# Row loads in a lane of their own in an induced-attention and leaky-FFN kernel

## The chip, the core and the metric

The kernel runs on one core of one Trainium2 chip. The metric is device time in microseconds (us), from launch to end. Engines are named as in the profile: PE is TensorE's matmul, PEld its weight load, DVE VectorE, ACT ScalarE, POOL GpSimd, SP the SyncE queue that issues the DMAs.

## The reference, cut to what matters

```python
B, N, m, C = (4, 12480, 32, 128)          # x: B x N x C, inducing: m x C, d_ff = 2048
def mab(q, kv):
    s = scale * (q @ kv.transpose(0, 2, 1))
    s = s - s.max(-1, keepdims=True)
    a = np.exp(s)
    a /= a.sum(-1, keepdims=True) + 1e-09
    return a @ kv
h = mab(I, x)                             # 32 inducing rows look at all 12480 rows of a block
attn = mab(x, h)                          # every row looks back at the 32 rows of h
hid = attn.reshape(B * N, 128) @ w_in
out = np.maximum(0.01 * hid, hid) @ w_out
```

All is float32. The first `mab` of a block needs x twice: transposed for the scores, and as rows for the values product `a @ kv`.

## The kernel before, in words

**The long loop.** The output is made in 98 tiles of 512 tokens (one of 384), each in 16 steps of 128 hidden columns: 1568 steps. A step is four matmuls of 512 columns on PE: the hidden product `ph` (L686), and three products into `po` (L725) from `ghi` and `glo`, a high and a low part of the activated hidden values. ACT makes `ghi` (L699), DVE makes `glo` (L707). The product `ph` runs three steps ahead (`LOOK`), through three buffers. The tiles of block b stand one block after the other, and the attention of block b+1 is woven in between the steps of block b. Since PE takes its queue in order, anything in this queue that waits holds all that stands behind it.

**The lanes.** `for u in range(WOVEN, NT * NF)` issues a step and then calls `step()` on generators: `stores` (outputs), `stacking` (copies of the weights `A` for the coming tiles), `seconds` (the second softmax), `scores` (`first_scores`) and `values` (`after_h`). A generator runs to its next `yield`. A yield of `HEAVY` (15) adds to `debt`, which falls by 5 in a step (6 while tiles of block 0 run); while it is above zero, most lanes stand still. `scores` and `values` also run only every second step.

**A block's first `mab`.** Its rows lie in six groups of 2048 and a small one of 192 (`RG`), visited in three passes, `PASSES = [[RG, 0, 1], [2, 3], [4, 5]]`. `first_scores` loads x for the scores, already in blocks of 32 columns (tile `xc`, by `load_blocks`, L227: 8 DMAs for half a group, 12 for the small group, three such sets at the start of a block: 28 DMAs), transposes on DVE, and at a visit makes the scores `s_ps`, their maxima (`peaks`), the running maximum `nm` and the exponentials on ACT (`running`, L303). `first_values` loads the same x as rows (tile `xr`, by `load_rows`, L217, one DMA of 256 KB for a quarter of a group, 16 buffers), turns the exponentials (tile `ay`), and marks the pass `ready`. `value_products` (L416) multiplies `ay` with the rows into `h_ps`: 64 matmuls, 66 where the small group takes part. It is called for pass p-1 in the visit of pass p, and for the last pass out of `first_values`.

**What sets the order around the row loads.** All these DMAs are issued by SP in the order in which the generators emitted them. In `first_values` the loads of a pass stand in the generator just ahead of its exponentials: `load_rows` and a `yield` for each quarter, then the wait until `(b, p)` is in `summed`, then the turning. `scores` begins the next block, with its 28 loads, as soon as it has made its last pass.

Of the kernel before, what the change touches and what calls it, by code (L numbers as in the profile page):

```python
# [20 lines left out]
def induced_attention_then_leaky_ffn(  # L21
# [103 lines left out]

    ring = set()
    PASSES = [[RG, 0, 1], [2, 3], [4, 5]]
    scores, early, ready, summed = [], {}, set(), {}
    rows_live, rows_made = set(), [0]
    waiting = []  # L130

    xT, xr, ex, aT, A4, hw, maxima, sums_of = {}, {}, {}, {}, {}, {}, {}, {}

# [77 lines left out]
    def load_rows(b, g, q):  # L211

        _, J, K = GROUPS[g]
        n = min(K, 4)
        t = row_tile("xr", (b, g, q))
        src = rows_of(b, g).rearrange("(p k) c -> p k c", k=K)
        nc.sync.dma_start(t[: 32 * J, :n, :], src[:, 4 * q : 4 * q + n, :])  # L217
        xr[b, g, q] = t

    def load_blocks(b, g, j0, nj):  # L220

# [49 lines left out]
    def running(b, p, rm):  # L271
        gs = PASSES[p]
        n = len(gs)
        nm_old = maxima.get(b)
        nm = sb.tile([P, 1], F32, tag="nm", name="nm", bufs=3)
        four = sb.tile([M, 12], F32, tag="rd", name="four", bufs=2)
        al = None
        for j in range(4):
            nc.gpsimd.tensor_scalar_mul(four[:, n * j : n * j + n], rm[32 * j : 32 * j + 32], -SCALE)
        yield  # L280
        if nm_old is None:
            nc.vector.tensor_reduce(out=nm[:M], in_=four[:, : 4 * n], op=ALU.min, axis=AX.X)
        else:
            least = sb.tile([M, 12], F32, tag="least", name="least", bufs=2)
            nc.vector.tensor_scalar(
                out=least[:, : 4 * n], in0=four[:, : 4 * n], scalar1=nm_old[:M], scalar2=None,
                op0=ALU.min, op1=ALU.min, accum_out=nm[:M],
            )
        for j in range(1, 4):
            nc.gpsimd.tensor_copy(nm[32 * j : 32 * j + 32], nm[:M])  # L290
        maxima[b] = nm
        yield
        if nm_old is not None:
            al = sb.tile([P, 1], F32, tag="al", name="al", bufs=4)
            nc.scalar.activation(al, nm_old, AF.Exp, bias=nm, scale=-1.0)
        zg = sb.tile([P, 3], F32, tag="zg", name="zg", bufs=2)
        if RG in gs:
            nc.vector.memset(zg[:, :1], 0.0)
        for i, g in enumerate(gs):
            _, J, K = GROUPS[g]  # L300
            w, rows = 32 * K, 32 * J
            e = ex[b, g]
            nc.scalar.activation(  # L303
                e[:rows, :w], e[:rows, :w], AF.Exp, bias=nm[:rows], scale=SCALE,
                accum_out=zg[:rows, i : i + 1],
            )
            if g != RG:
                yield
        zs = sb.tile([P, 1], F32, tag="zs", name="zs", bufs=2)
        nc.vector.tensor_reduce(out=zs, in_=zg[:, :n], op=ALU.add, axis=AX.X)  # L310
        if al is not None:
            old, one = sums_of[b], zs
            zs = sb.tile([P, 1], F32, tag="zn", name="zn", bufs=2)
            nc.vector.tensor_scalar(
                out=zs, in0=old, scalar1=al, scalar2=one, op0=ALU.mult, op1=ALU.add
            )
        sums_of[b] = zs
        summed[b, p] = al
# [20 lines left out]
    def first_scores(b):  # L339


        halves = [(RG, 0, 3)] + [(g, j0, 2) for g in range(RG) for j0 in (0, 2)]
        blocks = {}

        def more():
            if halves:
                h = halves.pop(0)
                blocks[h] = load_blocks(b, *h)

        for _ in range(3):  # L350
            more()
        yield from idle(10 if b > 1 else 4)
        for p, gs in enumerate(PASSES):
            for g in gs:
                _, J, K = GROUPS[g]
                w = 32 * K
                if g == RG:
                    xT[b, g] = t = sb.tile([P, J, w], F32, tag="xTr", name="xTr", bufs=2)
                else:
                    while len(ring) == RING:  # L360
                        yield
                    ring.add((b, g))
                    xT[b, g] = t = sb.tile([P, J, w], F32, tag="xT", name="xT", bufs=RING)
                for j in range(J):
                    if g == RG:
                        if j:
                            continue
                        nc.vector.transpose(
                            t.rearrange("p j w -> p (j w)"),
                            blocks[RG, 0, 3][:, : J * K, :].rearrange("p n c -> p (n c)"),  # L370
                        )
                    else:
                        blk = blocks[g, j - j % 2, 2][:, (j % 2) * K : (j % 2 + 1) * K, :]
                        nc.vector.transpose(t[:, j, :], blk.rearrange("p n c -> p (n c)"))  # L374
                    yield HEAVY
                    if j % 2 or g == RG:
                        more()
            while p and (b, p - 1) not in ready:
                yield
            while b - 1 not in hw or hw[b - 1][2] is None or not room(2):  # L380
                yield
            if p:
                value_products(b, p - 1)
            for q in [waiting.pop(0) for _ in range(min(2, len(waiting)))]:
                ps = gen_ps("s2_ps")
                second_scores(b - 1, q, ps)
                turned(b - 1, q, ps)
            sps = {}
            for g in gs:
                if g == RG:  # L390
                    sps[g] = ps_s.tile([P, TOK], F32, tag="hp", name="s1_ps")
                else:
                    sps[g] = aux_ps("s1_ps")
                for j in range(GROUPS[g][1]):
                    columns_product(sps[g], indT, b, g, j)
            rm = peaks(b, p, sps)
            yield HEAVY
            yield from running(b, p, rm)
            yield

# [36 lines left out]

    def first_values(b):

        todo = quarters(b)  # L440
        hacc = None
        for p, gs in enumerate(PASSES):
            for _ in range(sum(max(1, GROUPS[g][2] // 4) for g in gs)):
                while not room():
                    yield
                load_rows(*todo.pop(0))
                yield
            while (b, p) not in summed:
                yield
            for g in gs:  # L450
                _, J, K = GROUPS[g]
                rows = 32 * J
                e = ex.pop((b, g))
                if g == RG:
                    ay = sb.tile([P, K, M], F32, tag="ayr", name="ayr", bufs=1)
                else:
                    ay = sb.tile([P, 16, M], F32, tag="ay", name="ay", bufs=2)
                nc.vector.transpose(ay[:rows, :K, :].rearrange("p k m -> p (k m)"), e[:rows, : 32 * K])
                ays[b, g] = ay
                yield HEAVY if g != RG else 0  # L460
            ready.add((b, p))
            if p == len(PASSES) - 1:
                value_products(b, p)
                yield
            while (b, p) not in hps:
                yield
            hacc = gathered(b, p, hacc)
            yield
        rz = sums(b)
        yield  # L470
        yield from normalise(b, hacc, rz)
# [136 lines left out]
    def stack(tiles_, engine=None):  # L608
# [22 lines left out]
        for t, parts in tiles_:  # L631
            A4[t] = a4 = sb.tile([P, TOK], F32R, tag="A4", name="A4", bufs=A4_BUFS)
            to = 0
            for b, g, js in parts:
                w, o = 32 * GROUPS[g][2], at[b, g]
                for j in js:
                    for r in range(4):
                        nc.sync.dma_start(  # L638
                            a4[32 * r : 32 * r + 32, to : to + w].bitcast(F32),
                            (ahi, alo)[r % 2][32 * j : 32 * j + 32, o : o + w].bitcast(F32),  # L640
                        )
                    to += w
                yield

    tiles = []
    PAIR_AT = 4
# [25 lines left out]
            return tile_, tile_  # L672
        return tile_.rearrange("p (n a) -> p a n", a=2), tile_.rearrange("p (a n) -> p a n", a=2)

    live, accs = {}, {}
    slots = [
        (t, f) for f0 in range(0, NF, TURN) for t in range(QUICK) for f in range(f0, f0 + TURN)
    ]
# [116 lines left out]
                debt[0] += got  # L795

    def after_h(b):
        yield from first_values(b)
        yield from expand_weights(b)
        yield from expand_linear(b)  # L800
# [381 lines left out]
    with tc.manual_schedule():  # L1182
# [14 lines left out]
        for u in range(WOVEN, NT * NF):  # L1197
# [4 lines left out]
            ffn_second(u)  # L1202
            if f == NF - 1:
                stores.append(store(t))
            debt[0] = max(0, debt[0] - (5 if b else 6))
            if not debt[0]:
                step(stores)
            step(stacking)
            if not debt[0]:
                step(seconds)  # L1210
            if u >= max(due[0], 52) and not debt[0]:
# [44 lines left out]
```

## Time and profile before

| | us |
|---|---|
| median of 3 runs | 1544.31 (1543.95 to 1544.94) |
| the profiled execution | 1542.42 |
| its span, first to last instruction | 1540.2 |
| PE busy in the span | 1485.9 (96%) |
| DVE busy | 1267.2 (82%) |
| ACT busy | 1002.0 (65%) |
| POOL busy | 112.7 (7%) |

The median compares kernels; the profile tells where the time lies in one execution. Its span is 2.2 us shorter than its own time. PE's busy share is high because nearly all its work is one dense stream of equal matmuls; its idle time is best found by asking what it waited for, and then by looking at the queue it waited on.

### The profile page before, as it was taken

The numbers are of one execution on the slowest core, as the hardware profiler recorded it, in microseconds if no ns is written. First come the engines' busy times: TensorE is split into PE (matmuls) and PEld (weight loads), VectorE is DVE, ScalarE is ACT, GpSimd is POOL, SyncE is SP. The second block draws the span as 40 slices with busy tenths as digits, with TensorE's granted clock in tenths as the row PEclk, the third lists the DMA queues.
The fourth block names the chain that finished last, engine by engine and source line by source line (L and its number), as shares of the span: only waits on it lengthen the run. The fifth ranks groups of instructions, "written<-read, shape, count | busy, mean of one in ns | idle before, by whom it ended". The sixth has DMA issues, their size and how long they took to land.

```text
span 1540.2 us, 22252 instructions
## 1 busy us (share of the span) xinstructions
PE 1485.9 (96%) x7861; PEld 1261.3 (82%) x7861; DVE 1267.2 (82%) x2137; ACT 1002.0 (65%) x1748; POOL 112.7 (7%) x182
## 2 busy tenths in 40 slices
PE   8999999969999999599999999999999999999998
PEld 6788888858789787387888888888888898888887
DVE  7889889748889797398889888888888888888886
ACT  6666767636676565276766666766766666666665
POOL 1200100000110100010100100000001000000000
PEclk9999999989999999799999999999999999999999
DMA  8136543343435343344443233112212122122211
GB/s 277 42 68 113 106 83 76 90 88 59 83 77 90 74 88 76 57 79 89 87 91 77 69 76 76 41 22 48 43 21 52 23 39 49 33 37 41 42 28 21
DMA packets 402079, 105.23 MB, mean 68 GB/s; under 512 B 372624, under 2 KB 375088, under 8 KB 401968
## 3 DMA queue, kind: packets, MB, share of 16 engines
q1 hardware_dynamic: 401920, 103.80, 32.9%
q8 instruction: 62, 1.02, 0.3%
q14 instruction: 49, 0.40, 0.1%
q10 hardware_dynamic: 48, 0.02, 0.0%
HBM read 48.94 MB, written 25.56 MB: 48 GB/s over the span
## 4 chain that ended last, share of the span: by engine, by line
PE 90%; SPq 3%; DMA 2%; DVE 2%; ACT 1%; issue 1%; POOL 0%; DVEq 0%; ACTq 0%
PE po L725 63%; PE ph L686 22%; PE s_ps L241 2%; SPq L227 2%; DMA xr<-in_x_dram 2%; PE po L744 1%; PE h_ps L416 1%; DVE glo L707 1%; DMA raw<-in_moe_w_out_dram 0%; ACT ghi L699 0%; DMA raw<-in_moe_w_in_dram 0%; SPq L772 0%; ACT e L303 0%; SPq L638 0%; PE hw_ps L527 0%
## 5 line engine op out<-in xcount | busy, mean ns | idle before, releaser
L699 ACT ACTIVATE ghi<-ph 128x512 fp32r<-128x512 f32 (+1 forms) x1568 | 930.9, 596 | 504.3 <-PE ph L686 499.1
L707 DVE SCALAR_TENSOR_TENSOR glo<-ph,ghi 128x512 fp32r<-128x512 f32 (+1 forms) x1568 | 1043.7, 680 | 230.2 <-ACT ghi L699 207.8
L686 PE MATMUL ph<-A,hws 128*128 128x512 f32 (+1 forms) x1600 | 598.7, 378 | 4.9 <-DVE glo L707 4.5
L725 PE MATMUL po<-ghi,w_hi 128*128 128x512 f32 (+1 forms) x1568 | 594.5, 379 | 0.0
L725 PE MATMUL po<-glo,w_hi 128*128 128x512 f32 (+1 forms) x1568 | 593.7, 379 | 0.0
L725 PE MATMUL po<-ghi,w_lo 128*128 128x512 f32 (+1 forms) x1568 | 593.5, 379 | 0.0
L686 PEld LDWEIGHTS ph<-A,hws 128*128 128x128 f32 x1600 | 302.4, 189 | 66.0 <-DVE glo L707 12.4
L725 PEld LDWEIGHTS po<-glo,w_hi 128*128 128x128 f32 x1568 | 296.9, 189 | 42.1 <-DVE glo L707 0.7
L725 PEld LDWEIGHTS po<-ghi,w_lo 128*128 128x128 f32 x1568 | 296.7, 189 | 41.3
L725 PEld LDWEIGHTS po<-ghi,w_hi 128*128 128x128 f32 x1568 | 297.0, 189 | 39.9 <-ACT ghi L699 0.2
L754 DVE STREAM_TRANSPOSE osb<-po 128x512 f32<-128x512 f32 (+1 forms) x98 | 68.9, 703 | 1.5 <-PE po L744 1.5
L626 POOL TENSOR_TENSOR alo<-aT,ahi 128x512 fp32r<-128x512 f32 x22 | 28.2, 1280 | 573.7 <-ACT ahi L621 516.4
L416 PE MATMUL h_ps<-xr,ay 128*32 128x128 f32 x576 | 20.6, 287 | 36.2 <-DMA xr<-in_x_dram 36.1
L374 DVE STREAM_TRANSPOSE xT<-xc 128x512 f32<-128x512 f32 x72 | 50.5, 702 | 0.0
L416 PEld LDWEIGHTS h_ps<-xr,ay 128*32 128x32 f32 x576 | 14.9, 112 | 42.1 <-DMA xr<-in_x_dram 39.1
L579 POOL TENSOR_TENSOR y<-y,mx 128x512 f32<-128x512 f32 x23 | 24.2, 1051 | 257.5 <-DVE mx L577 202.8
L744 PE MATMUL po<-A,m2s 128*128 128x512 f32 (+1 forms) x100 | 37.1, 374 | 0.0
L594 POOL TENSOR_TENSOR y<-y,sm 128x512 f32<-128x512 f32 x23 | 24.2, 1050 | 174.2 <-DVE sm L592 143.3
L334 DVE STREAM_TRANSPOSE y<-s_ps 128x512 f32<-128x512 f32 x22 | 15.7, 715 | 13.7 <-PE s_ps L241 12.2
L241 PE MATMUL s_ps<-xT,indT 128*32 128x512 f32 x192 | 24.2, 595 | 0.5 <-ACT xT L851 0.5
L241 PE MATMUL s_ps<-xT,hT 128*32 128x512 f32 x192 | 24.0, 597 | 0.4 <-ACT hT L993 0.4
L744 PEld LDWEIGHTS po<-A,m2s 128*128 128x128 f32 x100 | 18.9, 189 | 2.6
(152 smaller groups left out, 370.0 us busy)
## 6 DMA issues: line engine op xcount, KB each, us to landing
xr<-in_x_dram SPq DMA_DIRECT2D x96, 256.0 KB, 4.4
out_dram<-osb SPq DMA_DIRECT2D x384, 64.0 KB, 2.2
xc<-in_x_dram SPq DMA_DIRECT2D x288, 64.0 KB, 2.7
A<-ahi SPq DMA_DIRECT2D x188, 64.0 KB, 2.0
A<-alo SPq DMA_DIRECT2D x188, 64.0 KB, 2.0
hws<-hilo SPq DMA_DIRECT2D x64, 64.0 KB, 2.0
raw<-in_moe_w_in_dram SPq DMA_DIRECT2D x4, 512.0 KB, 7.6
raw<-in_moe_w_out_dram SPq DMA_DIRECT2D x4, 512.0 KB, 8.3
```

The lines of the kernel that those rows point to most:

```text
L227: nc.sync.dma_start(t[32 * cb : 32 * cb + 32, j * K : (j + 1) * K, :], src[:, j0 + j, :, 32 * cb : 32 * cb + 32],)
L241: nc.tensor.matmul(dst, lhsT, rhs, start=True, stop=True)
L374: nc.vector.transpose(t[:, j, :], blk.rearrange("p n c -> p (n c)"))
L416: nc.tensor.matmul(hp[32 * k : 32 * k + 32, :C], ay[:rows, 4 * q + k, :], xb[:rows, k, :], start=(i == 0 and q == 0), stop=(last[k] == i a ...
L579: engines[0].tensor_tensor(out=yv, in0=yv, in1=mx[:rows, :K].unsqueeze(2).broadcast_to([rows, K, M]), op=ALU.subtract,)
L626: (engine or nc.gpsimd).tensor_tensor(out=alo[sl], in0=aT.pop((b, g))[: 32 * J, :], in1=ahi[sl].bitcast(F32), op=ALU.subtract,)
L686: nc.tensor.matmul(ph[:, o : o + w], hw[b][1][:, f * P : (f + 1) * P], woven(A4[t][:, o : o + w], t), start=True, stop=True,)
L699: nc.scalar.activation(halves(ghi[:, :n], t)[1], live[u][2], AF.Relu)
L707: nc.vector.scalar_tensor_tensor(out=halves(glo[:, :n], t)[1], in0=ph, scalar=0.0, in1=halves(ghi[:, :n], t)[1].bitcast(F32), op0=ALU.max, ...
L725: nc.tensor.matmul(accs[t][:, :n], w[:, f, :], woven(r[:, :n], t), start=(f == 0 and w is w_hi and r is live[u][0]), stop=False,)
L744: nc.tensor.matmul(accs[t][:, o : o + w], hw[b][2], woven(a4[:, o : o + w], t), start=False, stop=(o + w == n),)
L754: nc.vector.transpose(osb[:, :n], po[:, :n])
```

## The change

`first_values` no longer loads rows. A new generator `fetch` does, in a lane `fetches` that is stepped on odd steps from 52 on, whatever `debt` is. It emits the nine loads of the first pass of a block as soon as `after_h` begins, and the sixteen of the two other passes after the second visit of that block, each where one of the 16 buffers is free. `fetched` keeps the step of a pass's last load, and `landed` says whether all loads of a pass were emitted at least `LAND` (12) steps ago; a values product now waits for that in the planner. In `running` the memset of `zg` moves to the front, one more `yield` stands between the running maximum and the first `Exp`, and the small group's `Exp` gets a yield too. The visit waits for two free row buffers only if two second products wait. `debt` falls by 4 (5 in block 0) in a step, and a stack ends with three idle steps.

```diff
+    PASS_OF = {g: p for p, gs in enumerate(PASSES) for g in gs}
+    LAND = 12
...
+    visited, fetched, now = set(), {}, [0]
...
         xr[b, g, q] = t
+        fetched[b, PASS_OF[g]] = now[0]
+
+    def fetch(b):
+
+        for p, gs in enumerate(PASSES):
+            while p and (b, 1) not in visited:
+                yield
+            for g in gs:
+                for q in range(max(1, GROUPS[g][2] // 4)):
+                    while not room():
+                        yield
+                    load_rows(b, g, q)
+                    yield
+
+    def landed(b, p):
+
+        n = sum(max(1, GROUPS[g][2] // 4) for g in PASSES[p])
+        return sum((b, g, q) in xr for g in PASSES[p] for q in range(4)) == n and now[0] >= fetched[b, p] + LAND
...
         nm_old = maxima.get(b)
+        zg = sb.tile([P, 3], F32, tag="zg", name="zg", bufs=2)
+        if RG in gs:
+            nc.vector.memset(zg[:, :1], 0.0)
...
         yield
+        yield
         if nm_old is not None:
...
-        zg = sb.tile([P, 3], F32, tag="zg", name="zg", bufs=2)
-        if RG in gs:
-            nc.vector.memset(zg[:, :1], 0.0)
...
-            if g != RG:
-                yield
+            yield
...
-            while p and (b, p - 1) not in ready:
+            while p and not ((b, p - 1) in ready and landed(b, p - 1)):
                 yield
-            while b - 1 not in hw or hw[b - 1][2] is None or not room(2):
+            while b - 1 not in hw or hw[b - 1][2] is None or not room(min(2, len(waiting))):
                 yield
...
+            visited.add((b, p))
             rm = peaks(b, p, sps)
...
-        todo = quarters(b)
         hacc = None
         for p, gs in enumerate(PASSES):
-            for _ in range(sum(max(1, GROUPS[g][2] // 4) for g in gs)):
-                while not room():
-                    yield
-                load_rows(*todo.pop(0))
-                yield
...
             if p == len(PASSES) - 1:
+                while not landed(b, p):
+                    yield
                 value_products(b, p)
...
+        yield from idle(3)
...
     def after_h(b):
+        fetches.append(fetch(b))
         yield from first_values(b)
...
-            debt[0] = max(0, debt[0] - (5 if b else 6))
+            debt[0] = max(0, debt[0] - (4 if b else 5))
...
+            now[0] = u
+            if u >= 52 and u % 2:
+                step(fetches)
```

How the instructions stand on the engines, before and now. In the names `xr` is a load of rows, `xc` a load of x for the scores, `A` a copy for a coming tile, `out_dram` a store. A row with xN at its end stands for N in a row. The change's line numbers are those of its own file.

SP, block 1, last loads of rows before the block's last values product; before:

```order
L217 DMA xr<-in_x_dram 128x512 x3
L772 DMA out_dram<-osb 256x2x32 x4
L217 DMA xr<-in_x_dram 128x512 x5
L772 DMA out_dram<-osb 256x2x32 x4
L227 DMA xc<-in_x_dram 32x2x32 x12
L227 DMA xc<-in_x_dram 32x16x32 x16
L217 DMA xr<-in_x_dram 128x512 x3
L638 DMA A_4268<-ahi 32x512
```

Three of the rows' loads stand behind the 28 loads of the next block. SP, block 1, the sixteen loads of the passes two and three; now:

```order
L248 DMA xc<-in_x_dram 32x16x32 x24
L791 DMA out_dram<-osb 256x2x32 x4
L220 DMA xr<-in_x_dram 128x512 x4
L791 DMA out_dram<-osb 256x2x32 x4
L220 DMA xr<-in_x_dram 128x512 x8
L791 DMA out_dram<-osb 256x2x32 x4
L220 DMA xr<-in_x_dram 128x512 x4
L248 DMA xc<-in_x_dram 32x16x32 x8
```

All sixteen now stand ahead of the block's own last `xc` loads. Farther down the same queue, the 28 loads of the next block; now:

```order
L656 DMA A_3533<-alo 32x512
L791 DMA out_dram<-osb 256x2x32 x12
L248 DMA xc<-in_x_dram 32x2x32 x12
L248 DMA xc<-in_x_dram 32x16x32 x16
L791 DMA out_dram<-osb 256x2x32 x4
```

The next load of rows in the queue belongs to block 2. SP, block 2, the same place; before:

```order
L217 DMA xr<-in_x_dram 128x512
L638 DMA A_7594<-ahi 32x512
L638 DMA A_7594<-alo 32x512
L638 DMA A_7594<-ahi 32x512
L638 DMA A_7594<-alo 32x512
L227 DMA xc<-in_x_dram 32x2x32 x12
L227 DMA xc<-in_x_dram 32x16x32 x16
L217 DMA xr<-in_x_dram 128x512 x3
L772 DMA out_dram<-osb 256x2x32 x8
```

and now, the last load of rows of block 2:

```order
L791 DMA out_dram<-osb 256x2x32 x8
L248 DMA xc<-in_x_dram 32x16x32 x8
L791 DMA out_dram<-osb 256x2x32 x4
L220 DMA xr<-in_x_dram 128x512
L791 DMA out_dram<-osb 256x2x32 x4
L656 DMA A_7482<-ahi 32x512
```

Sixteen copies `A` and twelve stores stand between it and the 28 `xc` loads of block 3. ACT, the exponentials of the first pass of block 2 (`er` is the small group, `y` the second softmax of block 1); before:

```order
L621 CAST ahi<-aTr 96x64 x2
L699 ACTIVATE ghi<-ph 128x512 x9
L303 ACTIVATE er,zg<-er,nm 96x64
L303 ACTIVATE e,zg<-e,nm 128x512
L699 ACTIVATE ghi<-ph 128x512 x2
L585 ACTIVATE y<-y 128x512
L303 ACTIVATE e,zg<-e,nm 128x512
L699 ACTIVATE ghi<-ph 128x512 x25
```

and now:

```order
L639 CAST ahi<-aTr 96x64 x2
L718 ACTIVATE ghi<-ph 128x512 x10
L325 ACTIVATE er,zg<-er,nm 96x64
L718 ACTIVATE ghi<-ph 128x512
L603 ACTIVATE y<-y 128x512
L718 ACTIVATE ghi<-ph 128x512
L325 ACTIVATE e,zg<-e,nm 128x512
L718 ACTIVATE ghi<-ph 128x512 x4
L325 ACTIVATE e,zg<-e,nm 128x512
```

At least one `ghi` now stands between any two of the extra activations.

## Rows read from the trace of the kernel before

**Rows 1.** The page: busy time of PE, and PE's clock in 40 slices.

```profile
PE 1485.9 (96%) x7861; PEld 1261.3 (82%) x7861; DVE 1267.2 (82%) x2137; ACT 1002.0 (65%) x1748; POOL 112.7 (7%) x182
PEclk9999999989999999799999999999999999999999
```

**Rows 2.** Waits of PE: engine, line, releaser, us in total, times, longest.

```profile
PE h_ps L416 <- DMA xr<-in_x_dram: 36.1, 5, 20.8
PE ph L686 <- DVE glo L707: 4.5, 8, 1.4
```

**Rows 3.** Stretches: length; busy PE, PEld, DVE, ACT, POOL; PEclk; DMA share; GB/s.

```profile
320.08:336.25 16.17, 3.20 (x65) 1.64 (x65) 0.57 (x1) 0.35 (x1) 1.92 (x5) 0.66 0.66 138
336.25:339.45 3.20, 3.20 (x13) 2.58 (x10) 1.35 (x3) 1.20 (x2) 0.00 (x0) 0.56 0.18 44
503.80:508.39 4.59, 2.19 (x66) 1.65 (x67) 0.69 (x1) 0.06 (x1) 0.00 (x0) 1.00 0.63 144
613.00:637.01 24.01, 3.19 (x65) 1.64 (x64) 0.69 (x1) 0.06 (x1) 0.00 (x0) 0.62 0.43 84
637.01:640.02 3.01, 3.01 (x13) 2.47 (x9) 1.31 (x2) 1.07 (x2) 0.00 (x0) 0.60 0.00 0
878.52:880.30 1.78, 1.78 (x66) 1.78 (x69) 0.69 (x1) 0.06 (x1) 0.01 (x1) 1.00 0.00 0
804.23:806.00 1.77, 1.77 (x66) 1.77 (x67) 0.69 (x1) 0.05 (x1) 0.00 (x0) 1.00 0.17 39
```

**Rows 4.** Timeline of SP's issues around the first stall: start, us, queue, line.

```profile
311.01 18.84 SPq L227 DMA_DIRECT2D xc<-in_x_dram  x28
329.89 1.57 SPq L217 DMA_DIRECT2D xr<-in_x_dram  x3
```

**Rows 5.** The same around the second and the third stall.

```profile
499.94 3.51 SPq L772 DMA_DIRECT2D out_dram<-osb  x4
503.49 1.30 SPq L217 DMA_DIRECT2D xr<-in_x_dram  x2
...
612.72 18.29 SPq L227 DMA_DIRECT2D xc<-in_x_dram  x28
631.05 1.56 SPq L217 DMA_DIRECT2D xr<-in_x_dram  x3
```

**Rows 6.** Timeline of PE behind the first stall: idle and its releaser in brackets.

```profile
333.85 1.40 PE L416 MATMUL h_ps<-xr,ay 128*32 128x128 f32 x16 [12.47 <-DMA xr<-in_x_dram]
...
339.45 0.38 PE L686 MATMUL ph<-A,hws 128*128 128x512 f32 x1
...
340.31 0.38 PE L686 MATMUL ph<-A,hws 128*128 128x512 f32 x1
```

**Rows 7.** The view of the tile `xr`: its DMAs' landing.

```profile
DMA to landing us min/median/max: 2.3/4.4/7.2
```

**Rows 8.** Timeline of ACT at exponentials that waited.

```profile
164.79 0.35 ACT L303 ACTIVATE er<-er,nm 96x64 f32<-96x64 f32 x1 [1.44 <-DVE zg L298]
...
300.79 0.30 ACT L295 ACTIVATE al<-nm 128x1 f32<-128x1 f32 x1 [0.70 <-POOL nm L290]
...
436.98 0.35 ACT L303 ACTIVATE er<-er,nm 96x64 f32<-96x64 f32 x1 [0.84 <-DVE zg L298]
```

**Rows 9.** Stretches from PE's last matmul ahead of a wait for `glo`, columns as above.

```profile
165.43:167.20 1.77, 0.38 (x3) 0.00 (x1) 0.75 (x2) 1.77 (x5) 0.00 (x0) 1.00 0.54 88
302.31:303.05 0.74, 0.38 (x2) 0.00 (x1) 0.74 (x2) 0.74 (x2) 0.00 (x0) 1.00 0.00 0
438.36:442.77 4.41, 3.51 (x14) 2.11 (x12) 3.22 (x6) 4.01 (x9) 0.00 (x0) 1.00 0.28 73
```

**Rows 10.** The page's groups: busy us, mean ns of one, idle before, releaser.

```profile
L699 ACT ACTIVATE ghi<-ph 128x512 fp32r<-128x512 f32 (+1 forms) x1568 | 930.9, 596 | 504.3 <-PE ph L686 499.1
L707 DVE SCALAR_TENSOR_TENSOR glo<-ph,ghi 128x512 fp32r<-128x512 f32 (+1 forms) x1568 | 1043.7, 680 | 230.2 <-ACT ghi L699 207.8
L374 DVE STREAM_TRANSPOSE xT<-xc 128x512 f32<-128x512 f32 x72 | 50.5, 702 | 0.0
```

More of the change, by code (lines that the diff above doesn't have):

```diff
@@ L673, in halves @@
         return tile_.rearrange("p (n a) -> p a n", a=2), tile_.rearrange("p (a n) -> p a n", a=2)
-    live, accs = {}, {}
+    live, accs, fetches = {}, {}, []
     slots = [
```

## The prediction

> **What bounds the kernel now.** I read the page's first two parts first: PE is busy for 1485.9 of 1540.2 us, and its clock dips in the slices around 320 and 630 us alone [rows 1]. A dense engine in order is the bound, so its idle time is what a change can win. The list of PE's waits comes next: 36.1 us of them are `h_ps` waiting for the DMA of `xr`, and the next entry is 4.5 us, `ph` waiting for `glo` [rows 2]. The reader is to see that one line holds nearly all of it.
>
> Then I cut the timeline where these waits lie. A values product of 64 or 66 matmuls that waits for nothing takes 1.78 or 1.77 us; three took 16.17, 4.59 and 24.01 us [rows 3]. I call them A (block 1, last pass), B (block 2, first pass) and C (block 2, last pass). Why the rows were late is in SP's queue: ahead of A, SP issued the next block's 28 loads for 18.84 us, and only then the last three loads of rows, from 329.89 on [rows 4]; PE went on 3.96 us after that, at 333.85 [rows 6]. C is the same, 28 loads for 18.29 us and the three loads at 631.05; at B the last two loads stood behind four stores of 3.51 us [rows 5]. So these are waits for SP's order, not for bandwidth: the DMA engines were busy for 0.66, 0.63 and 0.43 of these stretches [rows 3].
>
> The 4.5 us lie mostly in four places, three of them shown, where ACT was held by an `Exp`: `er` waited for the memset of `zg` on DVE, for 1.44 and 0.84 us, or `al` waited 0.70 us for POOL's copies of `nm`; the `ghi` behind it on ACT was late, so was `glo`, and `ph` had no free buffer [rows 8].
>
> **The change part by part.** All terms go against the profiled execution, 1542.42 us, of which 2.2 us lie outside the span.
>
> *The lane of loads.* The 25 loads of a block stay; only their place moves. In A the stretch falls from 16.17 to 1.78, which gives 14.39; B gives 4.59 - 1.77 = 2.82; C gives 24.01 - 1.78 = 22.23 [rows 3]. Behind A and C PE ran two steps at a granted clock of 0.56 and 0.60, in 3.20 and 3.01 us [rows 3]: a mean over its two levels, 1.2 and 2.4 GHz, after standing still. A step takes 0.86 us by two `ph` in a row, 339.45 and 340.31 [rows 6], so two cost 1.72, and 1.48 and 1.29 come back as well. Behind B the clock had stayed at 1.00, so nothing is added there. Together 14.39 + 2.82 + 22.23 + 1.48 + 1.29 = 42.2 us.
>
> Does all of it go? That rests on how early the loads now stand. Following the lanes through the code step by step, I find the smallest distance between the last load of a pass and its product in block 1, pass two: loaded by step 203, multiplied at step 251. That is 48 steps of 0.86 us, 41 us. (The others: 54 and 57 steps for the last passes of the blocks 1 and 2, where A and C lie, and more.) Against this stands the longest burst of the queue, 18.84 us [rows 4], and the slowest landing, 7.2 us [rows 7]: 26 us. In the order of the change no burst of 28 stands between a load and its product. So I take the whole 42.2; if one burst and one slow landing met a pass in any way I have not seen, the 15 us left still cover it. The bound below is one stall left in place, that is a rival.
>
> What the loads are moved past: on SP they now stand ahead of some `xc` loads and `A` copies. A load of rows costs SP about 0.5 us (three in 1.57) [rows 4], so sixteen cost 8 us and hold those back by as much. A copy is issued from a stack that starts some 30 steps, 26 us, ahead of its tile, and its sixteen issues at about 0.65 take 10; 8 more still fit. At 0, then, hidden by the tile stream; without that cover it would be up to 8 us for each of three blocks.
>
> *The pauses at ACT's waits.* The memset moves ahead by several steps, and a lane's turn goes by between `nm` and the first `Exp`; since `scores` runs every second step at most, that is two steps or more, 1.7 us, against the longest such wait of 1.44 [rows 8]. The three `Exp` of a first pass now have `ghi` between them. What it is worth, from PE's own stretches: 1.77 less one matmul of 0.22 is 1.55; 0.74 - 0.22 = 0.52; 4.41 less thirteen matmuls, 2.81, is 1.60 [rows 9]. The last has a twin in block 3 of 4.42. Sum 1.55 + 0.52 + 1.60 + 1.61 = 5.3. What is late next is ACT's extra work itself: ACT needs 0.60 of a step for `ghi` [rows 10] and has 0.26 left, so two extra activations that meet still make a `ghi` late. The three steps that `ph` is ahead take that up. Bounds: 0 if other meetings of the same size arise, 5.3 if none do. I take 5.0, near the upper end, since the order of the change shows the activations apart and the waits at their heads gone.
>
> *Less DVE work between blocks.* A heavy DVE step is 0.70 us, `glo` 0.68 of a step of 0.86 [rows 10]. That leaves 0.18 in a step; a pay-off in four steps instead of three leaves 0.72 instead of 0.54 for 0.70 of work. PE shows no wait for DVE alone in the long stretches, so I put it at 0, between 0 and the 4.5 of [rows 2] that the term above has already taken. It costs time in the lanes: the weights of block 3 come 90 steps later (step 969 instead of 879), 18 later in block 2, 14 earlier in block 1. Their tiles start at steps 1168, 784 and 384, so this is covered by 199, 178 and 100 steps. The idle steps after a stack and the looser test for buffers have no wait of PE behind them in the trace: 0.
>
> Sum: 42.2 + 5.0 = 47.2 us, 1542.42 - 47.2 = 1495.2 in the profiled execution. The median of the runs stands 1.89 above that execution, so 1497.1; I round up to 1498 for meetings on ACT and DVE that I can't see.
>
> **The rivals.** *The transfers are short, not the issues.* The sixteen loads share the DMA engines with the `xc` loads; moved, they would land late at another place. For it: a DMA share of 0.66 in A [rows 3]. Against it: a third was free even there, and no load took over 7.2 us [rows 7]. If it were so, only the time from the last issue to its landing would come back in each stall, 3 x 4.4 by the median [rows 7], 13.2 us; with the 5.0: 1526. The Trainium skill, page "DMA: Bandwidth & Descriptors", section "Issuing engines are not separate DMA queues", speaks for this rival: it says that the time a sequencer takes to start a DMA is usually small relative to the DMA itself. The trace does not agree here: 28 issues took 18.84 us, longer than any landing of rows.
>
> *One stall stays.* If a pass meets a late load after all, most likely in block 2, whose last load waits longest for a free buffer (emitted at step 537, the one before it at 493), C keeps its 22.23 + 1.29: 1498 + 23.5 = 1521.5. The 57 steps to its product, 49 us, speak against it.
>
> *New meetings.* The longer lanes put second softmax, `A` splits and `Exp` together at other steps. Four of the size of those now lost, 1.3 us on average, would give 1503; eight 1508.
>
> *Slower: the blocks' chains run out of slack.* All 16 row buffers now fill early, the second softmax draws on the same buffers, and each block's chain comes later. Were block 3's weights late for step 1168, PE would stand still until they come, in one piece. It decides only from 199 steps (171 us) of further delay on; to end slower than before, another 47 us must come on top: a queue held for over 218 us. With those, 1550. Nothing in the order shows such a hold.
>
> *It doesn't do what it says*: the loads are emitted early, but SP holds each for its buffer until near the product. Then A, B and C stay and only the 5 goes: 1539, or 1544 without that.
>
> **How the numbers follow.** My forecast with its new meetings: 0.86 (1498, from 1495 to 1508). One stall stays 0.05; transfers 0.03; does nothing 0.03 (half of it within the bound); slower 0.03. The range reaches from 1494.5, the full 5.3 and a little of what other meetings cost now, to 1508, where eight new meetings end; it leaves out the other cases. A measurement of this kernel can tell about 0.2%, 3 us, from no change. Faster: 0.86 + 0.05 + 0.03 + 0.01 = 0.95; same 0.02; slower 0.03.
>
> **What would show it.** In the profile of the changed kernel: no wait of `h_ps` for `xr` in PE's list, or less than 1 us; nine values products of 1.8 us each; a clock without the two dips; `er` and `al` with no idle time ahead of them that DVE or POOL ended; a span near 1495. An `xr` wait of several us on PE proves the first step wrong; waits of `ph` for `glo` of more than 4.5 us prove the second wrong; a wait for `A` or `hws` on PE means that the chains' slack was misjudged.

## The result, and the profile after

| | before | after |
|---|---|---|
| median (range) | 1544.60 us (1543.95 to 1544.94, 4 runs) | 1495.55 us (1495.54 to 1496.72, 4 runs) |
| ratio | | 0.9685 [0.9668, 0.9702] |
| the profiled execution / its span | 1542.42 / 1540.2 | 1496.72 / 1494.6 |

The change makes the kernel 49 us faster; 1498.0 had been forecast. The page's busy line and clock line, which answer to [rows 1]:

```profile
PE 1480.1 (99%) x7861; PEld 1262.8 (84%) x7861; DVE 1265.5 (85%) x2137; ACT 999.6 (67%) x1748; POOL 112.4 (8%) x182
PEclk9999999999999999999999999999999999999999
```

PE is busy for 99% of a span that is 45.6 us shorter, and both dips of the clock are gone. PE's list of waits (engine, line, releaser, us in total, times, longest) has no `h_ps` that waits for `xr`; these are its first and its third entry, against the 36.1 and 4.5 of [rows 2]:

```profile
PE mx_ps L906 <- DVE onerd L897: 1.9, 2, 1.8
...
PE ph L705 <- DVE glo L726: 1.3, 2, 1.1
```

The first belongs to the start of the kernel, which the change doesn't touch. The three stretches A, B and C, in the columns of [rows 3]:

```profile
308.97:310.85 1.88, 1.88 (x65) 1.68 (x64) 0.69 (x1) 0.06 (x1) 0.00 (x0) 1.00 0.65 102
483.61:485.39 1.78, 1.78 (x67) 1.78 (x68) 0.69 (x1) 0.00 (x0) 0.00 (x0) 1.00 0.71 110
608.18:610.06 1.88, 1.88 (x65) 1.68 (x64) 0.69 (x1) 0.05 (x1) 0.00 (x0) 1.00 0.62 100
```

They took 16.17, 4.59 and 24.01. All nine values products now take 1.77 to 1.89. The DMA share in A and C is 0.65 and 0.62, where it was 0.66 and 0.43 [rows 3]: the DMA engines are about as busy there as before or busier, and the waits went all the same. SP's timeline in block 1 (start, us, queue, line) shows the sixteen loads of the passes two and three:

```profile
234.31 2.05 SPq L220 DMA_DIRECT2D xr<-in_x_dram  x4
236.99 2.62 SPq L791 DMA_DIRECT2D out_dram<-osb  x4
239.66 4.17 SPq L220 DMA_DIRECT2D xr<-in_x_dram  x8
...
254.06 1.99 SPq L220 DMA_DIRECT2D xr<-in_x_dram  x4
```

The second pass is complete with the fourth of the eight, at about 241.7, and its product starts at 285.55: 44 us, where the prediction worked out 41 for its smallest distance. The last of all is issued 53 us ahead of A.

**One correction of the base.** The first hidden product started at 52.48 us in this execution and at 50.37 in the one before:

```profile
52.48 0.70 PE L705 MATMUL ph<-A,hws 128*128 128x512 f32 x2 [0.22 <-ACT A L1097]
```

```profile
50.37 0.70 PE L686 MATMUL ph<-A,hws 128*128 128x512 f32 x2 [0.21 <-ACT A L1077]
```

(The first line is of after, the second of before.) The work ahead of it is the same, instruction for instruction; over all profiled kernels below the start lies between 50.4 and 52.8. (The six with the new lane start at 51.7 to 52.8, the four without it at 50.4 to 51.9. With one execution of each, whether the change has a part in that is not shown.) So I compare the rest, the span from the first hidden product on: 1540.2 - 50.37 = 1489.8 before and 1494.6 - 52.48 = 1442.1 after. The difference is 47.7, where the sum of the prediction was 47.2.

### The profile page after: what moved, and what is told of

Same layout as the page of the kernel before. It is cut to its first block, busy times and chain, and to the rows that moved or that the text cites. A ratio compares the mean times of both kernels' runs of the same rounds, so it can differ in the third digit from the quotient of the medians.

```text
span 1494.6 us, 22249 instructions
## 1 busy us (share of the span) xinstructions
PE 1480.1 (99%) x7861; PEld 1262.8 (84%) x7861; DVE 1265.5 (85%) x2137; ACT 999.6 (67%) x1748; POOL 112.4 (8%) x182
## 4 chain that ended last, share of the span: by engine, by line
PE 95%; DMA 2%; DVE 1%; SPq 1%; ACT 0%; issue 0%; POOL 0%; DVEq 0%; ACTq 0%
PE po L744 67%; PE ph L705 23%; PE s_ps L262 3%; PE po L763 1%; PE h_ps L438 1%; DMA xr<-in_x_dram 1%; DMA raw<-in_moe_w_out_dram 0%; DMA raw<-in_moe_w_in_dram 0%; SPq L248 0%; SPq L833 0%; PE w_ps L1069 0%; DVE glo L726 0%; ACT ghi L718 0%; DMA xc<-in_x_dram 0%; PE hw_ps L545 0%
## 5 line engine op out<-in xcount | busy, mean ns | idle before, releaser
L744 PEld LDWEIGHTS po<-ghi,w_lo 128*128 128x128 f32 x1568 | 296.3, 189 | 41.1
L280 DVE TENSOR_SCALAR_CACHE_REDUCE e<-s_ps 128x512 f32<-128x512 f32 x18 | 12.4, 690 | 8.3 <-PE s_ps L262 7.5
L438 PE MATMUL h_ps<-xr,ay 128*32 128x128 f32 x576 | 17.6, 274 | 0.0
```

The costliest lines, as they stand in the source:

```text
L438: nc.tensor.matmul(hp[32 * k : 32 * k + 32, :C], ay[:rows, 4 * q + k, :], xb[:rows, k, :], start=(i == 0 and q == 0), stop=(last[k] == i a ...
L744: nc.tensor.matmul(accs[t][:, :n], w[:, f, :], woven(r[:, :n], t), start=(f == 0 and w is w_hi and r is live[u][0]), stop=False,)
```

## The experiments

Three theories were to be told apart: that the order on SP alone made A, B and C (mine); that the transfers were what took long, or that a long lead was needed; and that the pauses or the pay-off of `debt` brought part of it. The last column is the span from the first hidden product on, of the one profiled execution.

| kernel | median us (range, runs) | ratio to before | from the first product on |
|---|---|---|---|
| before | 1544.67 (1541.95 to 1547.95, 13), then 1544.01 (1542.69 to 1546.40, 12) | 1 | 1489.8 |
| lane_only | 1502.27 (1501.89 to 1503.21, 4) | 0.9717 [0.9701, 0.9733] | 1448.7 |
| pauses_olddebt | 1542.97 (1539.86 to 1546.88, 10) | 0.9988 [0.9977, 1.0] | 1490.0 |
| after_olddebt | 1496.13 (1495.29 to 1496.75, 4) | 0.9678 [0.9663, 0.9692] | 1440.8 |
| xc_later | 1509.67 (1507.03 to 1510.56, 4) | 0.9763 [0.9748, 0.9777] | 1457.0 |
| act_queue | 1540.03 (1539.14 to 1541.46, 7) | 0.9972 [0.9962, 0.9983] | 1486.0 |
| latec0 | 1498.13 (1) | | 1444.0 |
| latec12 | 1496.17 (1) | | 1441.7 |
| fetch110 | 1495.68 (1493.74 to 1496.07, 5) | 0.9683 [0.9670, 0.9696] | 1441.1 |

### The lane without the pauses

lane_only is the change, with `running` and the pay-off as they were before and without the idle steps.

```diff
-        zg = sb.tile([P, 3], F32, tag="zg", name="zg", bufs=2)
...
-        yield
...
-        yield from idle(3)
...
-            debt[0] = max(0, debt[0] - (4 if b else 5))
+            debt[0] = max(0, debt[0] - (5 if b else 6))
```

> The change without its pauses and without its slower pay-off of debt: the memset of zg, the yields in running, the pay-off of 5 and 6 a step and the end of a stack are as before; the lane of loads, the landing rule and the looser test for free buffers stay. Theory (the rows stood late in SP's order): the three stalls and the slow clock behind two of them go, 42.2 us; the new wait of a transpose for an xc load in block 1, which cost PE 1.2 us in the profile of the change, may stay: 1502 to 1504, no wait of h_ps for xr. Rival (the transfers are what is short): only the landings come back, 13 us: 1531, with waits of h_ps for xr left.

The median fell by 42.4 us, and the span from the first product on by 41.1. A, B and C took 1.89, 1.78 and 1.88. PE's first wait and the wait of `er` on ACT are those of before:

```profile
PE ph L704 <- DVE glo L725: 4.0, 6, 1.4
```

```profile
ACT er L324 <- DVE zg L319: 3.1, 3, 1.4
```

So the lane carries its term of 42.2, within the spread of the runs, and nearly all the waits for `glo` are the other term's.

### The pauses without the lane

pauses_olddebt is the kernel before, with the pauses in `running`, the idle steps and the looser test for buffers; the loads stay in their old place.

```diff
+        zg = sb.tile([P, 3], F32, tag="zg", name="zg", bufs=2)
+        if RG in gs:
+            nc.vector.memset(zg[:, :1], 0.0)
...
+        yield
...
-            if g != RG:
-                yield
+            yield
...
+        yield from idle(3)
```

> The kernel before with the pauses alone: memset of zg at the front, one more yield ahead of the first Exp, a yield after the small group's Exp, three idle steps after a stack, the looser test for buffers; loads of rows where they were, pay-off of 5 and 6. Theory (ACT's waits for DVE and POOL made ghi and glo late): PE's four waits for glo shrink by about 5 us: 1539 to 1541, and the waits for xr stay near 36 us. Rival (the extra activations only meet elsewhere, or the stalls would have absorbed those waits): 1544, waits of ph for glo near 4.5 us.

This missed: 1.7 us instead of some 5, hardly above nothing (the interval of the ratio reaches to 1.0, and the span from the first product on is 0.2 us longer). PE's waits say why:

```profile
PE h_ps L416 <- DMA xr<-in_x_dram: 40.7, 6, 19.1
...
PE ph L687 <- DVE glo L708: 0.8, 1, 0.8
```

The waits for `glo` did fall, from 4.5 to 0.8 us. But the waits for `xr` grew from 36.1 to 40.7, nearly all of it at B, which took 8.74 us instead of 4.59. SP's timeline ahead of B:

```profile
485.93 11.63 SPq L227 DMA_DIRECT2D xc<-in_x_dram  x16
497.61 0.63 SPq L217 DMA_DIRECT2D xr<-in_x_dram  x1
498.34 2.64 SPq L773 DMA_DIRECT2D out_dram<-osb  x4
501.02 0.62 SPq L217 DMA_DIRECT2D xr<-in_x_dram  x1
```

PE reached B at 496.68, 7.1 us earlier than before, while the last load of rows was issued only some 3 us earlier: its last two loads stood behind sixteen `xc` loads, the very last behind four stores as well. Not all of the 7.1 us was won by the pauses: counted in `ph`, the product itself stands four steps, some 3.4 us, earlier in this program (483 instead of 487 ahead of it). And behind the longer wait the clock fell to its lower level, 1.2 GHz, which it had not done at B before:

```profile
505.42:507.00 1.58, 1.58 (x17) 0.92 (x14) 0.00 (x0) 0.00 (x0) 0.00 (x0) 0.50 0.00 0
```

So what the pauses won was waited away at the next late load. They are worth their microseconds only where nothing late stands behind them, and the two parts of the change don't simply add.

### The change with the old pay-off

after_olddebt is the change, with the pay-off of `debt` as before.

```diff
-            debt[0] = max(0, debt[0] - (4 if b else 5))
+            debt[0] = max(0, debt[0] - (5 if b else 6))
```

> The change with the pay-off of debt as before, 5 and 6 a step. Theory (the pay-off decides nothing for PE): 1495 to 1496, as the change. Rival (heavy DVE steps in closer order make glo late, and the slower pay-off is what took PE's waits for glo away): up to 4.5 us more, 1497 to 1500, with waits of ph for glo of some us.

1496.13 against 1495.55: nothing that can be told. The pay-off is worth 0 within that, as forecast. Against lane_only this kernel has the pauses and the idle steps after a stack, and nothing else: 1502.27 - 1496.13 = 6.1 us.

### Only the next block's loads held back

xc_later is the kernel before, with one condition: the first 28 `xc` loads of blocks 2 and 3 wait until the rows of the block ahead are all emitted. The loads of rows stay close to their products.

```diff
+        while b > 1 and b - 1 not in loaded:
+            yield
...
+            if not todo:
+                loaded.add(b)
```

> The kernel before, with one edit: the first 28 xc loads of blocks 2 and 3 are not emitted until all loads of rows of the block ahead are. No load of rows is moved to an earlier step. Theory (SP's order made the stalls A and C): they go, with the slow clock behind them, 14.39 + 1.48 + 22.23 + 1.29 = 39.4 us, and B stays at 2.8; the last loads now stand 8 and 10 steps, 7 to 9 us, ahead of their products, which a landing of 4 to 5 us and the issues ahead of it may use up, so up to 3 us stay at each: 1505 to 1511. Rival (the rows need the long lead of the new lane, or the transfers are short): half of A and C or more stays: 1520 or above.

35 us of the gain come from this alone. Stretches A, B, C and the one behind C:

```profile
320.73:322.62 1.89, 1.89 (x66) 1.69 (x65) 0.57 (x1) 0.35 (x1) 1.39 (x2) 1.00 0.09 13
488.30:493.32 5.02, 2.44 (x67) 1.80 (x69) 0.69 (x1) 0.06 (x1) 0.00 (x0) 0.91 0.66 138
599.16:604.52 5.36, 2.51 (x65) 1.50 (x64) 0.69 (x1) 0.06 (x1) 0.00 (x0) 1.00 0.60 175
604.52:607.97 3.45, 3.45 (x13) 2.83 (x10) 2.01 (x3) 1.19 (x2) 0.00 (x0) 0.58 0.10 16
```

A is gone, although its rows are loaded no earlier in the program than before; only the 28 loads ahead of them left. C keeps 5.36 us, and SP shows what stood there instead:

```profile
598.47 0.59 SPq L643 DMA_DIRECT2D A<-alo  x1
599.10 1.56 SPq L218 DMA_DIRECT2D xr<-in_x_dram  x3
```

The last three loads were issued behind a series of `A` copies at 599.10, and the product began at 599.16. This decides against the rival of short issues and long transfers, for which only some 13 us in all could come back. The Trainium skill, page "DMA: Bandwidth & Descriptors", section "Issuing engines are not separate DMA queues", holds the time to start a DMA to be usually small relative to the DMA itself. For one load of rows the trace agrees: about 0.5 us to issue (three in 1.57 [rows 4]) against 4.4 to land [rows 7]. The sum is what is long here: 28 starts on one queue took 18.84 us [rows 4], and the load that was due stood behind all of them. In the prediction I set the 28 starts against a single landing and took that for a disagreement, which compares unlike things; what speaks against the rival is the 35 us of this run.

The terms add up: A gives 14.3 + 1.5 of clock. C gives 24.01 - 5.36 = 18.7, but the clock behind it fell as before. B gives -0.4, and its clock fell too, about 1.3. That is some 32 to 33 us, and the span from the first product on is 32.8 shorter.

### The loads of rows on ACT's queue

act_queue is the kernel before, with the rows issued by ACT instead of SP, everything else in its place.

```diff
-        nc.sync.dma_start(t[: 32 * J, :n, :], src[:, 4 * q : 4 * q + n, :])
+        nc.scalar.dma_start(t[: 32 * J, :n, :], src[:, 4 * q : 4 * q + n, :])
```

> The kernel before with one word changed: the loads of rows of blocks 1 to 3 are issued by ACT's queue instead of SP's, at the steps where they were. Theory (the rows stood behind SP's other issues): they no longer wait for the 28 xc loads, so the waits of h_ps for xr fall from 36 us to under 8; ACT issues 75 loads between its activations, each perhaps 0.5 us (SP's price for one), against 0.26 us that ACT has left in a step, so ghi and glo come late in places: PE's waits for glo grow from 4.5 to between 5 and 20 us; 1505 to 1525 in all. Rival (the sixteen DMA engines are what is short): the waits for xr stay above 20 us, 1535 or above.

The part on `h_ps` came as expected: no wait for `xr`, and A, B and C took 1.88, 1.78 and 1.88, with the loads at the same steps of the program. So the wait was for SP's turn. The total missed, by far: 4 us were won. PE had new waits:

```profile
PE ph L686 <- DMA hws<-hilo: 17.8, 1, 17.8
PE ph L686 <- DVE glo L707: 15.0, 11, 5.1
```

The first is block 1's weights. SP's queue (its waits, then its timeline):

```profile
SPq L638 <- DMA xr<-in_x_dram: 24.8, 1, 24.8
```

```profile
414.56 0.58 SPq L638 DMA_DIRECT2D A<-ahi  x1
...
427.75 8.22 SPq L542 DMA_DIRECT2D hws<-hilo  x13
```

A copy of `A` on SP waited 24.8 us for a load of rows that ACT issued only near the end of that time, at 412.60 on ACT's timeline:

```profile
412.60 0.34 ACTq L217 DMA_DIRECT2D xr<-in_x_dram  x1
```

The sixteen copies and the weights stood behind it, and PE stopped at 413.7 until 431.86. The copy and the load share no data. What links them stands in the trace's records of the instructions: the load and the copy signal the same completion semaphore (the counter on which a DMA reports that it has landed), number 100, and SP's wait, which ends at 414.49, is for this number (and for one more); the load's last signal on it came at 414.47. SP had run ahead in its own queue, and was held until ACT reached the load at its place between the activations. It was not the only such wait. By SP's list for the whole kernel, `xc` loads, copies and stores waited for loads of rows for 161.7 us, in 31 places; the two largest entries:

```profile
SPq L227 <- DMA xr<-in_x_dram: 79.2, 16, 24.2
SPq L638 <- DMA xr<-in_x_dram: 64.4, 7, 24.8
```

In before no `xc` load, copy or store of the list waits for a load of rows. Most of the 15.0 us for `glo` lie behind transposes on DVE that waited 12.9 us for such late `xc` loads, by DVE's list of waits. So the miss came mostly from SP's holds, and not from ACT's time, which the expectation had counted.

The run also shows how short the cover of these weights was in the kernel before. There SP issued them at

```profile
416.26 11.01 SPq L542 DMA_DIRECT2D hws<-hilo  x16
```

and PE first used them at 427.14, 10.9 us after that. The hold of 24.8 us was longer than such a cover. Whether they would have been late with A gone and no hold isn't shown: in this run their issue would then have begun near 403, by subtraction, ahead of the 413.7 at which PE came for them. In the change they are all issued by 351.29, and first used at 412.19:

```profile
345.00 6.29 SPq L560 DMA_DIRECT2D hws<-hilo  x10
```

### The loads of C late again, without and with the landing rule

Both are the change, with block 2's last eight loads held until that pass is turned; once with no steps to wait in the rule `landed` (latec0: `LAND` 0; all loads must still be emitted) and once with its twelve (latec12, without the first two lines of the cut). Each was run once.

```diff
-    LAND = 12
+    LAND = 0
...
-            while p and (b, 1) not in visited:
+            while p and ((b, 1) not in visited or (b, p) == (2, 2) and (b, p) not in ready):
```

> The change with LAND at 0 and one gate: the eight loads of the last pass of block 2 are emitted only after that pass is turned, so from one step after the 28 xc loads of block 3, and the product is emitted three steps after the last of them, 18 steps after those xc loads. Theory (what counts is the distance from emission to product against SP's burst plus issue plus landing): the burst takes 18.3 us, eight issues 4, a landing 4 to 5, together some 27 us, against 18 steps of 0.86, 15.5 us: h_ps waits for xr by 8 to 13 us at that place alone, near 620 us, about 1506 to 1510 in all. Rival (a load that is emitted steps ahead has landed whatever stands ahead of it on SP): a wait of 3 us or less, 1496 to 1499.

> As the run with LAND at 0 and the gate on the last pass of block 2, but with LAND at 12: the product is emitted 30 steps, 26 us, after the 28 xc loads. Theory (distance against burst, issues and landing, 27 us): the wait falls by the twelve steps, 10 us, to between 0 and 3 us: 1495 to 1499. Rival (the landing rule gives nothing, since a product that comes later waits as long): the same wait as with LAND at 0.

Without the rule I had expected a wait of 8 to 13 us; the stretch C took 4.83, a loss of 2.95. The rival's number came out, but not its reason. SP's timeline ahead of it:

```profile
594.66 18.32 SPq L248 DMA_DIRECT2D xc<-in_x_dram  x28
613.02 1.09 SPq L220 DMA_DIRECT2D xr<-in_x_dram  x2
614.21 2.65 SPq L791 DMA_DIRECT2D out_dram<-osb  x4
616.90 4.45 SPq L220 DMA_DIRECT2D xr<-in_x_dram  x6
```

The 28 loads stand ahead of the rows on SP once more, and still they cost 3 us and not 22. They began at 594.66, 27.6 us ahead of the product at 622.30. I had counted from the step at which the planner emits them, 15.5 us ahead. SP didn't wait for that step: it issued the loads when the stores ahead of them were out, at 594.62. From there the theory's own sum fits: the last of the eight loads was issued by 621.35, 0.95 us ahead of the product, and no load of rows landed in under 2.6 us in this run. So it had not landed when the product began, against the rival, and it held the product until 627.13. With the rule the product came later in the program (633.81), and C took 1.88.

So the rule works where it is needed. In the change it isn't: with `LAND` 0 and nothing else changed, the program that is built is the same, instruction for instruction.

### A later start of the lane

One new cost had shown up in the profile after. DVE's timeline early in block 1's first `mab` (the bracket is idle time and its releaser), and PE's stretch there:

```profile
133.79 2.05 DVE L726 SCALAR_TENSOR_TENSOR glo<-ph,ghi 128x512 fp32r<-128x512 f32 x3
137.44 0.71 DVE L395 STREAM_TRANSPOSE xT<-xc 128x512 f32<-128x512 f32 x1 [1.60 <-DMA xc<-in_x_dram]
```

```profile
137.34:138.78 1.44, 0.38 (x2) 0.00 (x0) 1.34 (x3) 0.36 (x1) 0.00 (x0) 1.00 0.75 117
```

The nine early loads of rows hold back the `xc` loads behind them; a transpose waits 1.60 us, the `glo` behind it on DVE is late, and PE loses 1.44 - 0.22 = 1.22 us. So I started the lane later, when those `xc` loads are out (fetch110):

```diff
-            if u >= 52 and u % 2:
+            if u >= 110 and u % 2:
```

> The change with the lane of loads starting at step 110 instead of 52. Only the nine loads of block 1's first pass move; their product stands at step 188. Theory (they stood ahead of xc loads on SP, a transpose of xT waited 1.6 us for one at 137 us, and PE lost 1.2): that wait goes and nothing new comes, 1494 to 1495. Rival (the wait is one of the execution profiled, not of the order, or it moves to another transpose): the time of the change, 1495.5 to 1496.

The wait of `xT` is gone from DVE's list, and the profiled span from the first product on is 1.0 us shorter (1441.1 against 1442.1). The median is 1495.68 against 1495.55. A microsecond can't be told here, and no version beats the change by anything measurable. The size of this wait also differs between executions: by DVE's lists the same transpose waited 1.60, 1.23, 0.99, 0.69 and 0.30 us in five profiled kernels whose lane starts at 52 (after, lane_only, latec12, after_olddebt, latec0), and not at all in before and fetch110. So it belongs to the order, and PE's 1.22 us are its largest case.

## Why the prediction was right, point by point

**The bound and its place.** Right. PE in order was the bound, A, B and C were its idle time, and SP's order made them. lane_only, xc_later and act_queue remove the wait in three ways: loads earlier, other loads later, another queue.

**The lane's 42.2 us.** Right: 42.4 by the medians, 41.1 by the profiles, in which lane_only also carries the new cost of the next point (its `xT` waited 1.2 us for `xc`). The clock behind A and C came back with the waits.

**What the loads are moved past, put at 0.** Too low: 1.22 us in the profiled execution, less in the others. My step worked out the cover of the `A` copies (30 steps) and spoke of the `xc` loads in the same breath, with no cover worked out for them. They have the shorter one in block 1's first pass. My bound, up to 8 us for each block, held it.

**The pauses, 5.0 us with 5.3 as their upper end.** The mechanism was right, since `er` and `al` are gone from ACT's list of waits, but the size was too low: 6.1 to 6.7 (1502.27 less 1496.13 or 1495.55), and 7.9 and 6.6 by the spans from the first product on. By the medians the excess over my upper end, 0.8 to 1.4 us, is no larger than the spread of the runs. I took four places out of the eight waits of [rows 2] and left the others out. Two of them in the timeline of PE before:

```profile
399.36 0.48 PE L686 MATMUL ph<-A,hws 128*128 128x512 f32 x1 [0.38 <-DVE glo L707]
...
1173.82 0.48 PE L686 MATMUL ph<-A,hws 128*128 128x512 f32 x1 [0.66 <-DVE glo L707]
```

Measured as in [rows 9], from matmul to matmul, they cost 0.54 and 0.82 (gaps of 0.76 and 1.04 us less 0.22), and a third at 701.82 costs 0.28. With the first and the third 6.1 could be had; neither has a counterpart in after_olddebt, and the change itself keeps one of 0.23 us, at 937.3. The third, by DVE's timeline, stands behind two heavy DVE steps in a row, so the prediction's "no wait for DVE alone" was not quite true. The wait at 1173.82 was not the pauses' to win. Ahead of it, at 1172.15, ACT's cast into `ahi` had waited for a copy `A<-ahi`, and that wait is in ACT's lists of before and after alike:

```profile
ACT ahi L621 <- DMA A<-ahi: 1.8, 1, 1.8
```

```profile
ACT ahi L639 <- DMA A<-ahi: 1.4, 1, 1.4
```

PE's wait behind it stood at 0.87 us in lane_only and, in the five kernels with both lane and pauses, at anything from 0.27 (after) to 0.80 (latec12). Which of the pauses and idle steps took the other small waits away was not tried.

The two errors, the loads' cost and the pauses, have opposite signs and nearly cancel in the profiled execution: 47.7 against 47.2. That closeness is luck in part.

**Less DVE work, 0.** Right by after_olddebt. What the idle steps and the looser test for buffers bring apart from the pauses wasn't tried.

**Rounding up to 1498 for unseen meetings.** Not borne out: apart from the one of 1.2 us none came, and the median of 1495.55 is 1.5 us below the sum's 1497.1. The term that failed here is the 1.89 us by which I set the median above the profiled execution: it is one execution's distance from the others, and after the change it was -1.17 (1495.55 against 1496.72). In the profiled execution itself the kernel was 1.5 us slower than the sum's 1495.2, with a start 2.1 us later. The range and its side held.

**The rivals.** None came. The transfers did become slower to land, which that rival had said: 5.1 us in the median and 8.6 at most, where [rows 7] had 4.4 and 7.2.

```profile
DMA to landing us min/median/max: 2.6/5.1/8.6
```

With 44 us of lead nobody waits for it. The chains' slack was not touched. But I counted the cover of the weights in steps of the planner, and SP's timeline is what decides: block 1's weights were issued 10.9 us ahead of their first use in the kernel before, and 71 us ahead of it in the change (341.22 and 412.19).

## What to carry to other kernels

When a dense engine waits for a load, look at what its DMA queue issued just ahead of it before looking at bandwidth: a burst of small loads for work much later can stand in front of the one load that is due. Move the due load ahead of the burst, or the burst behind it, and then look at what the moved load now holds back and at the wait that was hidden behind the old one. Loads moved to another queue are not yet free of the first one: look whether the two share completion semaphores. Time won on another engine counts only if no late load stands between it and the end, so judge small gains after the large wait is gone.

## What the runs showed of the hardware that I had not expected

**A queue runs ahead of its place in the program.** In latec0 SP issued a burst 12 us ahead of the time that I had worked out from the step in which it was emitted.

**Two queues can hold each other.** In act_queue a copy on SP waited 24.8 us for a load that ACT issued, with no data in common but the same completion semaphore, number 100. That the two queues share it is a property of this program.

**The clock after a short wait.** Behind values products that took 4.59 us (B before) and 4.83 (C in latec0) PE's granted clock stayed at 1.00, the level of 2.4 GHz. Behind 5.02 and 5.36 (B and C in xc_later) and 8.74 (B in pauses_olddebt) it fell to 0.50, the lower level of 1.2 GHz; the rows behind B in the kernel before, behind C in latec0 and behind B in xc_later:

```profile
508.39:510.00 1.61, 1.61 (x28) 1.02 (x23) 0.28 (x1) 0.00 (x0) 0.00 (x0) 1.00 0.08 12
```

```profile
627.13:629.00 1.87, 1.87 (x13) 1.66 (x10) 0.69 (x1) 1.08 (x2) 0.00 (x0) 1.00 0.05 8
```

```profile
493.32:495.00 1.68, 1.68 (x17) 0.92 (x14) 0.00 (x0) 0.00 (x0) 0.00 (x0) 0.50 0.10 14
```

In xc_later the three steps behind C took 4.38 us, from the `ph` at 604.52 to the one at 608.90, where three steps at speed take 2.58:

```profile
604.52 0.48 PE L691 MATMUL ph<-A,hws 128*128 128x512 f32 x1
...
608.90 0.38 PE L691 MATMUL ph<-A,hws 128*128 128x512 f32 x1
```

So a wait of 3.5 us cost 1.8 us more behind it, no less than the 1.48 and 1.29 us behind the long stalls A and C of the kernel before. What decides whether the clock falls these runs don't show.
